# S4D convolution and gMLP mixer on one core: the cosine products of every generation unit on GpSimd, the last chunk's spectra in one part, a new instruction order

## The chip, the cores and the metric

The kernel runs on one core of a Trainium2 chip, in one launch. The metric is the device time of one execution in microseconds; runs are compared by their medians. PE is TensorE (PEld its weight loads), DVE is VectorE, ACT is ScalarE, POOL is GpSimd, SP is SyncE, which issues most of the DMAs.

## What is computed

Two residual blocks on one sequence of L = 2048 positions and D = 512 channels. The first is a diagonal state-space layer: each channel has a convolution kernel K made of 128 damped oscillations, and the layer convolves the normalized input with K by FFT. The second is a gMLP mixer with a 2048 x 2048 spatial weight.

```python
A = -exp(log_A_real) + 1j * A_imag;  C = (C_real + 1j * C_imag) * dt[:, None]
P = exp((A * dt[:, None])[:, :, None] * pos)          # 512 x 128 x 2048
K = 2 * einsum("dn,dnl->dl", C, P).real               # the generation
y = irfft(rfft(K, 4096) * rfft(u_t, 4096))[:, :L]
h = x + y + u * D_skip                                # u = layernorm(x)
z = gelu(layernorm(h) @ w_in);  z1, z2 = z[..., :896], layernorm(z[..., 896:])
out = h + (z1 * (w_sp @ z2 + b_sp)) @ w_out
```

## The kernel before

`phase_a` (lines 266 to 672) does the state-space layer up to the inverse transform over one axis; the phases `b1` to `b3` finish it and do the mixer. The change touches `phase_a` alone.

*The generation.* K is not built by exponentials of all 512 x 128 x 2048 elements. Position l is split in a coarse and a fine part, so that exp(a l) is a product of two factors with cosines and sines, and the sum over the 128 oscillations is a matmul. Each of 32 units (`unit(su)`, line 481) makes K for 16 channels:
- TensorE computes phases for the 16 channels, `c_k` times `sw` (2 matmuls of 512 columns, into a two-bank PSUM tile `ph`); ScalarE and VectorE reduce them to one turn in `cs` (part of the buffer `wb`).
- ScalarE takes the sine of all of it into a second two-bank tile, the absolute value of `cs`, and from that two cosines of 512 columns: `ce` into a PSUM bank, and `cw`.
- GpSimd makes three width factors `m` (part of `wa`, two sets, so units `su` and `su + 2` share one) out of the small tables `mt`.
- VectorE multiplies sines and width factors into `f3` (`f_94` to `f_96`). A group of 16 small matmuls, the unit's first product, starts `kp`. VectorE multiplies `ce` with two width factors in place (`wa<-ps,wa`, 1024 columns). `cw` times the third width factor is the left operand of the unit's second product, 16 more matmuls into `kp`.
- `kp` is copied to a small buffer `ks` (six of them) and GpSimd adds the skip term.

Before, where `cw` lies and who multiplies it goes by the parity of the unit (lines 499 and 525): in even units ScalarE leaves `cw` in SBUF and GpSimd multiplies (`wb<-wb,wa`), in odd units ScalarE writes it to a PSUM bank and VectorE multiplies from there (`wb<-ps,wa`).

*The transforms.* Channels come in four chunks of eight units. `piece_a` and `piece_b` transform the normalized input of a chunk (two FFT stages); `exchange` swaps the halves of its spectrum across partitions, two DMAs of 1 MB from SP, the second behind the first. `piece_c` takes the first stage of K, unit by unit, as the left operand `ks`, and evacuates to `big`. `piece_d(c, g, lo, n)` is K's second stage (left operand `big`, right operand `a2`) for the columns `lo` to `lo + n` of the eight units' 32; VectorE multiplies the result with the input's spectrum in place (`trio<-ps,trio`, always 1024 columns). `piece_e` is the inverse stage with `c_inv`: eight matmuls, which need the products of all of `piece_d` for their columns, and then an evacuation to `big` (all Q), which is what phase `b1` reads in its first matmul, `y` at line 748. The exchange of chunk c writes where `piece_e` of chunk c - 1 reads.

Before, the last chunk was split in two halves of columns, 0 to 15 and 16 to 31: four `piece_d` and four `piece_e` each. A half's `piece_d` has 8 matmuls of 64 columns, an unsplit one 4 of 128.

*What sets the order.* All of `phase_a` is first recorded (`Plan`), each instruction or group with a place in `RANKS`. `FORMS` picks the engine where a step may run on one of two (evacuations on ScalarE or VectorE, parameter steps on VectorE or GpSimd). `BANKS` picks the PSUM bank: two two-bank tiles (`ps_98`, `ps_99`) and four single banks (`ps_100` to `ps_103`). Sorted by rank, the steps are issued in that order on each engine's queue, and semaphores follow from the data. Everything recorded carries line 250 in the profile. Three tables written out as digits thus set the order; no planner runs in the kernel.

Of the kernel before, what the change touches and what calls it, by code (L numbers as in the profile page):

```python
# [12 lines left out]
AF = mybir.ActivationFunctionType  # L13
# [3 lines left out]
P = 128  # L17
# [8 lines left out]
KS_BUFS = 6  # L26
SLOT = 4096
WIDE = 2
EVERY = 2
SUC = 8  # L30
MAGIC = 12582912.0
TWO_PI = 2.0 * math.pi
# [34 lines left out]
BANKS = (
    "345242325433352143423545214452504241024301533511252002324002530153541153500454513444540422555312244155253325542112321132"
    "550042511524200223104222114331134452011043535413345514544522240544511323002434005541124251143001452201245002523545235425"
    "43212345422135332045255112430043341135311342200545113524004441124223250353252444523"  # L70
)


# [192 lines left out]
def phase_a(ctx, gen, tc, ins, cst, ident, c_mean, c_inv, Q, wp, scr):  # L266
# [214 lines left out]
    def unit(su):  # L481
# [27 lines left out]
        sn = ph[:, 1, :]  # L509
# [742 lines left out]
```

## Time and profile before

| | |
|---|---|
| median of 3 runs | 846.28 us (845.6 to 850.01) |
| the profiled execution | 844.69 us, its span 842.9 us |
| busy in the span | PE 794.1, PEld 685.6, DVE 654.2, ACT 469.1, POOL 278.5 us |
| `phase_a` ends | the first `y` matmul starts at 297.40 us |
| granted TensorE clock | full speed over nearly all of the span |

A row of a timeline has start, length, engine, line, operation, output<-input and how many instructions it merges. TensorE records two matmuls for each fp32 matmul of the program (eight `piece_e` matmuls are 16 records) and one for each phase matmul. A row that merges many instructions in close sequence is read by its length over their count. A row of the groups has busy time, mean of one in ns, and behind the second bar the idle time of the engine ahead of them with what ended it. The chain that ended last is followed back from the last instruction to whatever released each step.

### The profile page before, as it was taken

How to read it: one execution, taken by the hardware profiler on the slowest of the kernel's cores; microseconds unless marked ns; L12 is line 12 of the kernel's file. 1: busy time of each engine (PE TensorE's matmuls, PEld its weight loads, DVE VectorE, ACT ScalarE, POOL GpSimd, SP SyncE). 2: the span in 40 equal slices, each digit the busy share in tenths (PEclk: the TensorE clock that was granted, in tenths of full speed). 3: DMA queues.
4: the chain of work that ended last, by engine and by line, in shares of the span. 5: the costliest groups of instructions: out<-in, count | busy, mean ns of one | idle time of the engine just before them, and what ended most of it. 6: DMA issues, size and time to landing. Idle time of an engine off the chain costs nothing.

```text
span 842.9 us, 17463 instructions
## 1 busy us (share of the span) xinstructions
PE 794.1 (94%) x6813; PEld 685.6 (81%) x6813; DVE 654.2 (78%) x1260; ACT 469.1 (56%) x783; POOL 278.5 (33%) x332
## 2 busy tenths in 40 slices
PE   1388999999998999999999999999999999999998
PEld 0287889899997998888899988888887888888886
DVE  7999998999999488851367679988955985787633
ACT  5998999999897233543223345456534533454111
POOL 5778777787755000000042100324221002222200
PEclk9999999999999999999999999999999999999999
DMA  9231432302218676364175044899889558799832
GB/s 352 76 113 32 111 91 61 86 25 62 52 38 269 233 251 163 99 172 154 51 150 126 1 126 132 187 228 213 201 206 210 171 149 189 156 236 216 204 110 77
DMA packets 63875, 121.81 MB, mean 145 GB/s; under 512 B 6737, under 2 KB 21201, under 8 KB 61489
## 3 DMA queue, kind: packets, MB, share of 16 engines
q1 hardware_dynamic: 52160, 99.33, 38.9%
q0 software_dynamic: 11632, 21.37, 15.6%
q8 instruction: 53, 0.87, 0.4%
q14 instruction: 30, 0.24, 0.1%
HBM read 92.89 MB, written 19.40 MB: 133 GB/s over the span
## 4 chain that ended last, share of the span: by engine, by line
PE 67%; DVE 14%; DMA 7%; issue 6%; ACT 5%; POOL 1%; SPq 1%; DVEq 0%; ACTq 0%; POOLq 0%
PE ps L250 20%; PE m L1140 18%; PE pz L835 9%; PE pz L935 9%; DMA raws<-in_w_sp_dram 6%; PE po L1063 5%; DVE trio L250 4%; PE y L748 3%; PE pl L1063 2%; ACT wb L250 2%; DVE wts L676 1%; ACT big L250 1%; ACT ps L250 1%; DVE wb L250 1%; DVE f L250 1%
## 5 line engine op out<-in xcount | busy, mean ns | idle before, releaser
L1140 PE MATMUL m<-wts,zc_wa 128*128 128x512 f32 x700 | 218.0, 391 | 1.0 <-DVE c L1155 1.0
L1140 PEld LDWEIGHTS m<-wts,zc_wa 128*128 128x128 f32 x700 | 131.4, 188 | 29.8 <-DVE c L1155 1.5
L1140 PE MATMUL m<-wts,zc_wb 128*128 128x512 f32 x350 | 136.7, 391 | 0.0
L1011 POOL DMA_DIRECT2D raws<-in_w_sp_dram x64 | 58.1, 1009 | 209.2 <-DMA raws<-in_w_sp_dram 208.0
L250 POOL TENSOR_TENSOR wa<-mt 128x512 f32<-128x512 f32 x96 | 107.3, 1131 | 35.2 <-PE ps L250 15.6
L675 ACT CAST wts<-raws 128x512 fp32r<-128x512 f32 x112 | 68.8, 619 | 52.3 <-DMA raws<-in_w_sp_dram 31.7
L676 DVE TENSOR_TENSOR wts<-raws,wts 128x512 fp32r<-128x512 f32 x112 | 77.0, 690 | 19.6 <-ACT wts L675 19.5
L935 PE MATMUL pz<-w,ht 128*128 128x448 f32 x384 | 77.4, 363 | 0.0
L1140 PEld LDWEIGHTS m<-wts,zc_wb 128*128 128x128 f32 x350 | 65.7, 188 | 14.0
L935 PEld LDWEIGHTS pz<-w,ht 128*128 128x128 f32 x384 | 72.0, 188 | 5.3
L835 PE MATMUL pz<-ht,w1h 128*128 128x512 f32 x224 | 71.3, 395 | 0.0
L250 ACT ACTIVATE ps<-wb 128x512 f32<-128x512 f32 (+1 forms) x80 | 65.3, 825 | 3.4 <-DVE trio L250 1.3
L941 POOL TENSOR_SCALAR sm<-sm 128x1 f32<-128x1 f32 x16 | 5.5, 342 | 186.3 <-DVE sm L940 186.3
L250 PE MATMUL ps<-big,a 128*128 128x128 f32 (+1 forms) x512 | 62.4, 278 | 0.9 <-DVE trio L250 0.8
L675 ACT CAST zc_wa<-raws 128x384 fp32r<-128x384 f32 (+1 forms) x70 | 37.0, 533 | 46.8 <-DVE raws L1045 34.1
L1063 PE MATMUL po<-w,gz 128*128 128x512 f32 x252 | 62.6, 396 | 0.0
L250 PEld LDWEIGHTS ps<-big,a 128*128 128x128 f32 x512 | 59.3, 192 | 3.5 <-DVE trio L250 1.1
L250 PE MATMUL ps<-c_inv,trio 128*128 128x128 f32 x512 | 60.6, 277 | 1.3 <-DVE trio L250 1.3
L250 PEld LDWEIGHTS ps<-c_inv,trio 128*128 128x128 f32 x512 | 58.8, 192 | 3.2 <-DVE trio L250 1.9
L1063 PEld LDWEIGHTS po<-w,gz 128*128 128x128 f32 x252 | 47.3, 188 | 11.5 <-DVE zo L1103 0.4
L835 PEld LDWEIGHTS pz<-ht,w1h 128*128 128x128 f32 x224 | 42.1, 188 | 9.2
L1045 DVE TENSOR_TENSOR raws<-z 128x384 f32<-128x384 f32 (+1 forms) x80 | 46.1, 584 | 0.3
(162 smaller groups left out, 1533.0 us busy)
## 6 DMA issues: line engine op xcount, KB each, us to landing
raws<-in_w_sp_dram SPq DMA_DIRECT2D x112, 256.0 KB, 4.0
raws<-in_w_sp_dram POOLq DMA_DIRECT2D x80, 256.0 KB, 5.8
trio<-trio SPq DMA_DIRECT2D x8, 1024.0 KB, 6.9
g<-in_c_g_dram SPq DMA_DIRECT2D x8, 1024.0 KB, 6.7
scr_z<-zo SPq DMA_DIRECT2D x28, 256.0 KB, 2.3
big<-in_u_a_dram SPq DMA_DIRECT2D x8, 512.0 KB, 7.6
xq<-in_u_b_dram SPq DMA_DIRECT2D x4, 1024.0 KB, 6.7
scr_h<-xq SPq DMA_DIRECT2D x16, 256.0 KB, 4.9
```

What stands on the lines that cost most here:

```text
L250: r = getattr(getattr(self.nc, e), method)(*map(self.real, args), **{k: self.real(x) for k, x in kw.items()})
L675: nc.scalar.copy(hi, src)
L676: nc.vector.tensor_sub(lo, src, hi.bitcast(F32))
L748: nc.tensor.matmul(ys[n, g][:, i, :], gt[:, i, r, :], qv[:, r, l0 + i], start=(r == 0), stop=(r == 1))
L835: nc.tensor.matmul(pt, w[:, q, f], ht[n][k][:, q], start=(q == 0 and i == 0), stop=(q == 3 and i == 2))
L935: nc.tensor.matmul(pt[:, :FQ], a[:, q], w2[:, b, q, f], start=(q == 0 and i == 0), stop=(q == 3 and i == 2))
L941: nc.gpsimd.tensor_scalar_add(sm[:, 14:15], sm[:, 13:14], 1e-5)
L1011: nc.gpsimd.dma_start(r, ws[1], accum_op=ALU.add)
L1045: nc.vector.tensor_tensor(zs[:, :w], x, y, op=op)
L1063: nc.tensor.matmul(pt, gz[fb][x][:, P * a:P * a + P], wo[:, y, fb, w], start=(first and fb == fbs[0] and i == 0), stop=(last and fb == fbs ...
L1140: nc.tensor.matmul(pt, x[:, f], y, start=(k == 0 and i == 0), stop=(k == KT - 1 and i == 2))
```

## The change

Three things. In every unit `cw` stays in SBUF and GpSimd multiplies it; the PSUM bank of the odd units and their VectorE product are gone, and with them the constant `EVERY` and a branch that was never taken. The last chunk's `piece_d` and `piece_e` are recorded in one part like the other chunks': eight `piece_d` of 4 matmuls with 128 columns in place of eight with 8 of 64. And the three tables are new throughout. Line numbers fall by one where the constant is gone: recorded steps carry line 249.

```diff
-EVERY = 2
...
 RANKS = (
-    "05000608010709040B0F0A0R0M0V0I0f0Z0j03020C0E0G0H0J0K0L0O0Q0S0U0X0Y0a0N0b0d0m0g0l0o0r0u0z10121316181A1D1Y1O1a1d1h1t221w25"
...
+    "0600040901050F080B0A0b0Q0l0I0M070g0W03020C0E0G0H0J0K0L0N0O0R0V0Y0Z0c0U0d0e0n0i0m0q0t0w0z0+1112131416181J1T1w231+2628292D"
...
         nc.scalar.activation(cs, cs, AF.Abs)
-        if WIDE == 3:
-            co = nc.bank([P, 2, W], 3)
-            nc.scalar.activation(co, cs, AF.Sin, bias=half_pi, scale=-TWO_PI)
-            cw, ce = co[:, 0, :], co[:, 1:2, :]
-        else:
-            ce, cw = nc.bank([P, 1, W], 0), nc.bank([P, W], 0) if su % EVERY == 1 % EVERY else cs[:, 0, :]
-            nc.scalar.activation(ce, cs[:, 1:2, :], AF.Sin, bias=half_pi, scale=-TWO_PI)
-            nc.scalar.activation(cw, cs[:, 0, :], AF.Sin, bias=half_pi, scale=-TWO_PI)
+        ce, cw = nc.bank([P, 1, W], 0), cs[:, 0, :]
+        nc.scalar.activation(ce, cs[:, 1:2, :], AF.Sin, bias=half_pi, scale=-TWO_PI)
+        nc.scalar.activation(cw, cs[:, 0, :], AF.Sin, bias=half_pi, scale=-TWO_PI)
...
         nc.vector.tensor_mul(m[:, 0:2, :], ce.to_broadcast([P, 2, W]), m[:, 0:2, :])
-        if su % EVERY == 1 % EVERY:
-            nc.vector.tensor_mul(cs[:, 0, :], cw, m[:, 2, :])
-        else:
-            nc.gpsimd.tensor_tensor(cw, cw, m[:, 2, :], op=ALU.mult)
+        nc.gpsimd.tensor_tensor(cw, cw, m[:, 2, :], op=ALU.mult)
         with nc.group():
-            product(cs[:, 0, :], m[:, 0:2, :], 1)
+            product(cw, m[:, 0:2, :], 1)
...
-        split = [(0, 32)] if c + 1 < NCH else [(0, 16), (16, 16)]
-        for lo, m in split:
-            for g in range(NK1 // (1 << (P // m).bit_length() - 1)):
-                piece_d(c, g, lo, m)
-            for s in range(lo // 4, (lo + m) // 4):
-                piece_e(c, s)
+        for g in range(8):
+            piece_d(c, g, 0, 32)
+        for s in range(8):
+            piece_e(c, s)
```

In counts, by engine and within `phase_a`: TensorE has 2128 matmuls where it had 2160. VectorE has 454 instructions where it had 465: sixteen products fewer, four parameter steps and four `ks` copies fewer, 13 more evacuations of 512 columns. ScalarE takes as many evacuations fewer and four `ks` copies more, and loads its function table 19 times where it was 18. GpSimd has sixteen products and four parameter steps more. Everything behind `phase_a` is the same instructions in the same order.

The order at three places. First VectorE at the last two units, before. `f_94` and `f_95` are units 30 and 31; `wb<-wb,ps` reduces a unit's phases, `wa<-ps,wa` is its last multiplication, `trio<-ps,trio` a product of the last chunk's `piece_d`:

```order
L250 SCALAR_TENSOR_TENSOR wb<-wb,ps_99 128x1024
L250 TENSOR_TENSOR f_94<-ps_98,wa 128x512
L250 SCALAR_TENSOR_TENSOR f_94<-wa,ps_98 128x512
L250 COPY big<-ps_102 128x128x4
L250 TENSOR_TENSOR f_94<-ps_98,wa 128x512
L250 TENSOR_TENSOR f_95<-ps_99,wa 128x512 x2
L250 TENSOR_TENSOR wa<-ps_102,wa 128x1024
L250 TENSOR_TENSOR trio<-ps_100,trio 128x2x16x32
L250 TENSOR_TENSOR wb<-ps_102,wa 128x512
L250 SCALAR_TENSOR_TENSOR f_95<-wa,ps_99 128x512
L250 TENSOR_TENSOR wa<-ps_100,wa 128x1024
L250 TENSOR_TENSOR trio<-ps_98,trio 128x2x16x32
```

The same place now:

```order
L249 SCALAR_TENSOR_TENSOR wb<-wb,ps_99 128x1024
L249 TENSOR_TENSOR wa<-ps_102,wa 128x1024
L249 COPY big<-ps_98 128x128x4
L249 TENSOR_TENSOR f_95<-ps_99,wa 128x512
L249 SCALAR_TENSOR_TENSOR f_95<-wa,ps_99 128x512
L249 TENSOR_TENSOR f_95<-ps_99,wa 128x512
L249 TENSOR_TENSOR wa<-ps_102,wa 128x1024
L249 COPY big<-ps_101 128x128x4
L249 COPY big<-ps_102 128x128x4
L249 TENSOR_TENSOR trio<-ps_101,trio 128x64x16
L249 TENSOR_TENSOR trio<-ps_100,trio 128x64x16
```

The `wb<-ps` product of unit 31 and the `piece_d` product ahead of its last multiplication are gone; all eight `piece_d` products follow behind it, and two evacuations stand between.

Second, TensorE from the last two units to the inverse transforms of the last chunk, before (`f` and `wa,wb` are a unit's first and second product, `wb,ks` is `piece_c`, `big,a` is `piece_d`, `c_inv,trio` is `piece_e`):

```order
L250 MATMUL ps_102<-wb,ks_85 64x128 x8
L250 MATMUL ps_101<-big,a_78 128x4x16 x8
L250 MATMUL ps_100<-big,a_78 128x4x16 x8
L250 MATMUL ps_103<-big,a_78 128x4x16 x8
L250 MATMUL ps_98<-big,a_78 128x4x16 x8
L250 MATMUL ps_102<-f_94 32x64 x16
L250 MATMUL ps_102<-wa,wb 32x64 x16
L250 MATMUL ps_100<-f_95 32x64 x16
L250 MATMUL ps_100<-wa,wb 32x64 x16
L250 MATMUL ps_102<-wb,ks_80 64x128 x8
L250 MATMUL ps_100<-wb,ks_81 64x128 x8
L250 MATMUL ps_101<-c_inv,trio 128x128 x8
```

And now:

```order
L249 MATMUL ps_103<-wa,wb 32x64 x16
L249 MATMUL ps_98<-wb,ks_84 64x128 x8
L249 MATMUL ps_100<-f_95 32x64 x16
L249 MATMUL ps_100<-wa,wb 32x64 x16
L249 MATMUL ps_103<-wb,ks_80 64x128 x8
L249 MATMUL ps_102<-wb,ks_81 64x128 x8
L249 MATMUL ps_101<-big,a_78 128x4x32 x4
L249 MATMUL ps_100<-big,a_78 128x4x32 x4
L249 MATMUL ps_103<-big,a_78 128x4x32 x4
L249 MATMUL ps_102<-big,a_78 128x4x32 x4
```

Four of the eight `piece_d` stood ahead of the last two units' products; now all eight stand behind the last `piece_c`, and behind them the eight `piece_e`.

Third, TensorE at the last inverse transforms of chunk 2, which the last chunk's exchange waits for, before:

```order
L250 MATMUL ps_98<-c_k,sw_91 128x512 x2
L250 MATMUL ps_100<-c_inv,trio 128x128 x8
L250 MATMUL ps_103<-f_96 32x64 x16
L250 MATMUL ps_103<-wa,wb 32x64 x16
L250 MATMUL ps_102<-wb,ks_81 64x128 x8
```

And now:

```order
L249 MATMUL ps_100<-f_94 32x64 x16
L249 MATMUL ps_100<-wa,wb 32x64 x16
L249 MATMUL ps_98<-c_k,sw_91 128x512 x2
L249 MATMUL ps_101<-c_inv,trio 128x128 x8
L249 MATMUL ps_102<-wb,ks_82 64x128 x8
```

Before, the last inverse transform of chunk 2 stood ahead of the products of unit 26 (`f_96`); now it stands behind those of unit 27 (`f_94`), with four units still to come in place of six.

More of the change, by code (lines that the diff above doesn't have):

```diff
@@ new lines @@
+    "2E2H2K0y2J0-1K2N2P2b2X2e2V2j2u2z2p1Y1k1o2h2l2-0T0D0P0X0a0S0h0o0k0f331V371C10151W3c3N0s1O1c1r5X0j1p1l0p1j1n1q1g1D1B1U1P1m"
+    "1X1b1A0x1H0u1I1h1i0r0v1Z1G1F1a171E1Q1R1u1y222527212A2F2L2O2Q2S2U2W2Y2a2c2d2g2i3I2s3L3Y2m3K3W3M3G2w2+382v423F3Q3l2n4N3V3r"
+    "3q4P312r35323R3Z3A3D3T3y3p3O461v1f3B1-1S363E191e3C1x2t241s1z393H1N1d341M1L2q2x302M2G2o2R2I2y2k3J3P3g3k3m3X3s3t3x3z3-4043"
+    "4547494B4D4E4H4G4R4I4T544S4x4h4W4f4M4j4u4m514s4U4V5P4k4o4K4Q5H4r4e4+4X574p4L4c4J4O594Y5a5Z5T6E692C2f2Z3S3e3+414Z4d4g4i4l"
@@ new lines @@
+    "4n4t4w5A5C5I5L5U5i5n5l5s5u6P6T4A655O5R6a6l746-777A6t6r6w6+5F5M5d6I797G3b3v4C444F4b6d8u8+909194989A9L9O9d9V9f9o9kAfAhAjAv"
+    "AyB1BIAQB59GA5BOBxChCTCOCDC5CbC4CUCMC2CfCWCKCGC8CB9n9i9rAoEBEGBGEIEO555W585J4a4v5N5c5E5K4q4-52564z536U6c727C7n7s6G6N6368"
+    "6x767q7-7D7J848h3U3d3i505D5S5Y3f2T205G5B5Q5m5b5g5r608X8i8r3a3h3o5j5q5+5x3j1t2B625y5w6M6J5-6Q6V6k8E8N3n3u4y646B6S6L5o5v6C"
+    "6A6F6O6o6X6R6s707L979M3w61666i6v7873676Y6f717B6q7K7H7E7P7T7e9N9S7Q486K8m8w9T6D6W6g6n7F7W7Y6p756y6z7N7R7y7d7g818Q8a8d8o7I"
@@ new lines @@
+    "7O7V7b7h7x7v7M7Z7U7o7l7r88827z8B8G8k8x9C7f7k7u838H8L8q7t868A898C8K8-8R8z95999I9U9a7w878F8P8Z8g8l8S8M8I8c8Y8j8p8v8t92969B"
+    "9E9J7+7m8b939pA15z6b5h5p5V5f5t6H5e5k6Z6h6j6u6e6m7i7p7S7a8O8V8T8f7c7j7X808J8U858D9m9s9+A79qA2A6AA9g9vACAHA9AD9t9yAbAkAUAc"
+    "ALAnAwBNB2BFBTBcBhBsBMBkBpCZ9Z9e9lA4ABAGAK9c9Q9DAVARATAiAaAPAmArAxDBDKAFAJAMASAWAeAZ9Y9K9uAlAXAgBBAqAdBEBLBPCxD1ApAuA-B4"
+    "B6BSBCAYAsAzB7B9BDBaBUBJBdBiBrCnD4AtA+B3BVBXBjBgBABZBRBYBeBbCCBnC0CFCNCeE3ECDG9xB0BfB+EMB8BKBQBlBqCPBwBWBmBtB-BvBzC-CdCH"
@@ new lines @@
+    "D3D8DCDPDeBHCICRCcCjCvCsC9CQCXCmC+CuD5DACwDHDQDTDaDkCtCzD2D9DJDXDOCoDED6DYDNDFDjDdDbDlDsE5E8EHD7DDDSDZDgDqDmD0DVDMDrDoDi"
+    "DzDtDxE0E4E7EJESDICgDhEAETEk8W8n8e8s9F8y9H9z9P9R9W9X9b9j9hA3AEA89wA09-AIAOANBuCJBoC7CSCYCVCkCLCyC1CAByC3C6CEEcEjEVEbEYEd"
+    "EiEpEuEzEoEvEfEnElEtFlFtFdFrF3FDFSFbGTGbFKFYG1GNGHGPGcH9DfDyE2E9EDENEKERDpD-EZEQELEwEUEmEyF9FUGpGwDwE1E6ErExF7F1EXEFEaF8"
+    "F2F6FEFBF5FJFLFcGuGzEEEhFIFOFVFmFaEqF0FAFTFXFQFyFuFfF+G2G9GCGUFCFGFNFRFeFqFoFFFPFMFgFhFkFwFzFvG8GDGRGxH3FHEeFWFjGaGyFZFi"
@@ new lines @@
+    "FnFxG0G6GBFpG4GAG5GEGIGgGWGLGjGmGtHFHLFsG3G7GFGJGYGQF-GGGSGKGMGkH5GsGXH8HWHbHhHpGOGVGfGoH4HBHGH1GnGvH7H2G+HMHHHPHVHcHjHn"
+    "HvGlG-HAHIHNHYHSGdHEHKHOHRHTHdHgHeHmHoHrHtHzGrGhH6I7IDIMCiCrCqCaCpClDLDUDRDWD+DcDnDuDvEPEgEWE+F4EsE-HJHaGZGiIRIcH0HDGeGq"
+    "IOIUHQHXHwI3I0I5IFIQILISIIINIBIHI4IAI8IEIGIJIvJ2JuKCJ6JTJYJiJfJoIkJ7IYIgJNJxK2KfHZHfHkHqIKIWIPHUHsHlI2H-HyIfIbIVIiImIxKH"
+    "KNHCHiHuH+I6I9IdI1ICHxIjIXInJ0ItIhJ3J9JCKVKgITIZIeIlIpI+IuIaIsIzIqIyJ4JHJDJ1JLJOJRK0K7IrIwI-J5JBJGJQIoJ8JEJAJIJMJmJUJbJp"
@@ L70 @@
[L70 removed]
+    "345452345244335544523535253025554240055110423005311052211552013400044010433330224523313242203203321123325421144400252114"
+    "340055200435115230025311352524324022325345045255203254433350043210523113220045411434005231033511242203423245225454431323"
+    "5253334323511554004401154400223104201155200455114243534225443422535"
 )
```

34 lines of the change are left out of this document (6 added, 28 removed).

## The prediction

> **What bounds the kernel now.** I read the stretches of the execution first, then the chain that ended last, then TensorE's and VectorE's timelines around the end of the generation, and at last the grouped instructions up to 300 us. The table by stretch: its columns are the window, its length, and the busy time of PE, PEld, DVE, ACT and POOL.
>
> ```profile
> 56.00:121.50 65.50, 60.62 (x1113) 53.06 (x1105) 64.14 (x95) 61.20 (x88) 49.53 (x54) 1.00 0.40 105
> 121.50:250.00 128.50, 127.86 (x2221) 117.36 (x2223) 120.98 (x159) 119.58 (x148) 91.87 (x98) 1.00 0.23 52
> 250.00:275.00 25.00, 22.41 (x517) 19.40 (x511) 24.52 (x30) 19.90 (x29) 14.54 (x18) 1.00 0.85 260
> 275.00:297.40 22.40, 21.67 (x192) 21.48 (x192) 9.30 (x9) 6.28 (x11) 0.00 (x0) 1.00 0.53 206
> 297.40:842.90 545.50, 540.54 (x2565) 457.14 (x2565) 385.99 (x792) 217.92 (x421) 83.47 (x112) 1.00 0.64 161
> ```
>
> The change touches only what lies ahead of 297.4 us. There, three engines are nearly full at once. TensorE is busy for 127.86 of 128.5 us up to 250 us and VectorE for 24.52 of the 25 us behind that; ScalarE follows closely. GpSimd has the room: 91.87 of 128.5 us, 71%. Past 297.4 us TensorE is busy for 540.54 of 545.5 us, with an unchanged program, so I let that part move as a block. The chain that ended last (start, length, what):
>
> ```profile
> 169.00 80.70 PE ps L250 x1351
> ...
> 270.29 1.23 DVE wa L250
> 271.52 3.40 DVE trio L250 x3
> 274.97 21.72 PE ps L250 x192
> ```
>
> So the path runs through TensorE until 249.7 us, through VectorE for the last units of the generation, and through TensorE for the inverse transforms of the last chunk. The `wa` row at 270.29 us is the last multiplication of unit 31, the last unit; it ends at 271.52 us. From there to the end of the 192 matmul records, at 274.97 + 21.72 = 296.69 us, it takes 25.2 us. TensorE's timeline around this:
>
> ```profile
> 240.86 0.72 PE L250 MATMUL ps<-c_k,sw 96*128 96x512 f32 x2
> 241.42 1.95 PE L250 MATMUL ps<-c_inv,trio 128*128 128x128 f32 x16
> 243.30 0.65 PE L250 MATMUL ps<-f 128*32 128x64 f32 x32
> 243.77 0.63 PE L250 MATMUL ps<-wa,wb 128*32 128x64 f32 x32
> 244.33 2.05 PE L250 MATMUL ps<-c_inv,trio 128*128 128x128 f32 x16
> ...
> 246.67 1.95 PE L250 MATMUL ps<-c_inv,trio 128*128 128x128 f32 x16
> ...
> 263.03 7.36 PE L250 MATMUL ps<-big,a 128*128 128x64 f32 x64
> ...
> 274.97 3.84 PE L250 MATMUL ps<-c_inv,trio 128*128 128x128 f32 x32 [0.40 <-DVE trio L250]
> ...
> 287.52 9.15 PE L250 MATMUL ps<-c_inv,trio 128*128 128x128 f32 x80
> ```
>
> The row at 263.03 us is the first half of the last chunk's `piece_d`; it runs while unit 31 is still being made. The 0.40 us wait at 274.97 us is all that TensorE pays between the units and the inverse transforms.
>
> **The change, part by part.** The groups of the first 300 us (instructions, then busy us and mean ns of one, then the idle time ahead of them):
>
> ```profile
> L250 POOL TENSOR_TENSOR wa<-mt 128x512 f32<-128x512 f32 x96 | 107.3, 1131 | 35.2 <-PE ps L250 15.6 <-DVE wb L250 13.9 <-DVE trio L250 1.6
> L250 POOL TENSOR_TENSOR wb<-wb,wa 128x512 f32<-128x512 f32 x16 | 20.5, 1280 | 13.6 <-ACT wb L250 13.3 <-DVE big L250 0.2
> L250 POOL TENSOR_TENSOR ks<-ks,wb 128x4 f32<-128x4 f32 x32 | 6.6, 210 | 13.0 <-ACT ks L250 10.2 <-DVE ks L250 2.6
> L250 DVE TENSOR_TENSOR wb<-ps,wa 128x512 f32<-128x512 f32 x16 | 10.9, 684 | 0.6 <-ACT ps L250 0.5
> L250 DVE COPY ks<-ps 128x256 f32<-128x256 f32 x16 | 6.7, 418 | 0.6 <-PE ps L250 0.6
> L250 DVE TENSOR_TENSOR trio<-trio 128x128 f32<-128x128 f32 x5 | 1.5, 301 | 0.0
> L250 ACT ACTIVATE ps<-wb 128x512 f32<-128x512 f32 x48 | 32.5, 689 | 1.6 <-DVE trio L250 0.6 <-DVE wa L250 0.4
> L250 ACT ACTIVATE wb<-wb 128x512 f32<-128x512 f32 x16 | 11.5, 718 | 0.2
> L250 ACT COPY big<-ps 128x512 f32<-128x512 f32 x55 | 31.7, 580 | 18.4 <-PE ps L250 17.8
> ```
>
> And VectorE's timeline, where instructions that follow each other closely overlap by 0.08 us: the two `f` products start 0.60 us apart though each takes 0.68.
>
> ```profile
> 226.00 5.74 DVE L250 TENSOR_TENSOR trio<-ps,trio 128x1024 f32<-128x1024 f32 x5
> ...
> 239.56 1.28 DVE L250 TENSOR_TENSOR f<-ps,wa 128x512 f32<-128x512 f32 x2
> 240.76 0.68 DVE L250 TENSOR_TENSOR wb<-ps,wa 128x512 f32<-128x512 f32 x1
> ```
>
> *VectorE ahead of the last unit's multiplication.* Counted in the two orders, the sixteen `wb<-ps` products go (16 x 0.60 = 9.6 us). One `piece_d` product moves behind that point (5.74 / 5 = 1.15), four `ks` copies go to ScalarE (4 x 0.34 = 1.4) and four parameter steps to GpSimd (4 x 0.22 = 0.9). In return VectorE takes eight more evacuations of 512 columns from ScalarE (8 x 0.60 = 4.8). Sum: -13.0 + 4.8 = -8.2 us, in the stage where VectorE ends last.
>
> *ScalarE.* Sixteen sines go to SBUF for 718 ns instead of PSUM for 689 (+0.5 us), ten evacuations leave (-10 x 0.50), four `ks` copies come, and one more load of its function table: about -2 us. It was not last and stays so; I add nothing.
>
> *GpSimd.* Sixteen more products at 1280 ns are +20.5 us, the parameter steps about +1.8. Its queue idles 35.2 + 13.6 + 13.0 = 61.8 us ahead of these three groups alone, so the work fits. What is queued behind a product that waits for its sine are the width factors of later units and the `ks` additions, and VectorE and TensorE wait for those. The cost lies between 0 and the lateness worked out under the rivals; I take 0, by the 61.8 us.
>
> *The last chunk in one part.* Sixty-four records of 64 columns took 7.36 us, 115 ns each; eighty of 128 columns took 9.15 us, 114 ns each. Half the columns cost the same, so merging two halves takes away 64 records, 7.4 us of TensorE, ahead of 275 us. The price is at the end. All eight `piece_d` now stand behind the last unit, VectorE must multiply all eight before the first inverse transform, and no inverse transform of a first half is there to fill. ScalarE's copy of the last `piece_c`:
>
> ```profile
> 274.62 0.58 ACT L250 COPY big<-ps 128x512 f32<-128x512 f32 x1 [0.29 <-PE ps L250]
> ```
>
> From 271.52 to the end of this copy are 3.7 us, which stay. Then come one `piece_d` on TensorE (8 records, 0.9, and about 0.2 until VectorE starts), eight products of 1.15 (9.2) and 128 records of inverse transforms (14.6): 28.6 us where it was 25.2, so +3.4 us.
>
> *Sum*: -8.2 + 3.4 = -4.8 us, if TensorE lets VectorE run ahead. The check from TensorE's side: in the new order its last inverse transform of chunk 2 (before: ended at 246.67 + 1.95 = 248.6 us) has two more units' products and two more phase matmul pairs ahead of it: 2 x (0.47 + 0.56) + 2 x 0.56 = 3.2 us, giving 251.8. VectorE then still has twelve short and five long instructions up to unit 31's multiplication, 12 x 0.60 + 5 x 1.15 = 13.0, of which about 0.9 lie ahead: 251.8 + 12.1 + 28.6 = 292.5 against 296.7, -4.2 us. The two agree; I take -4.8. The profiled execution took 844.69 us with a span of 842.9, 1.6 us (0.2%) below the median of 846.28. Against its own time the sum gives 839.9, against the median 841.5, which is my forecast.
>
> [...]
>
> **The rivals.**
> *GpSimd holds the units up (slower).* In the odd units the second product of a unit now waits for GpSimd, 1.28 us in place of 0.68, and for what stands in its queue, one width factor of 1.13: 1.7 us late, 16 times, 27.7 us. Where half of that surfaces the kernel ends at 841.5 + 13.8 = 855.3. It is slower by over 0.5% from (4.8 + 4.2) / 27.7 = 33% on. For it: 15.6 us of GpSimd's waits already end on TensorE, because only two sets of width factors exist, and a late product delays the next set. Against it: its 61.8 idle us, and that a unit's two products stand units apart in the order. [...]
>
> *The last exchange comes late.* The two half swaps that the last `piece_d` need cannot start before chunk 2's last inverse transform:
>
> ```profile
> 248.69 7.98 SPq L250 DMA_DIRECT2D trio<-trio  x2
> ```
> ```profile
> trio<-trio SPq DMA_DIRECT2D x8, 1024.0 KB, 6.9
> ```
>
> The second is issued about 7.5 us behind the first and lands 6.9 later: 14.4 us. In the new order only units 28 to 31 stand between, 12.1 + 3.7 + 1.1 = 16.9 us. With 2.5 us of room, a TensorE that is 5 us late there costs 2.5 us: 844.0, within 0.5%.
>
> *The new order brings waits of its own.* Units 1 to 7 now follow each other with nearly equal work on all four engines; a few us of waits there, or a slower start, give 844 to 848, within 0.5%.
>
> *The start is shorter too.* Summed over the two orders with the same durations, VectorE has 1.6 us less to do ahead of the first `piece_a`, and TensorE gets chunk 1's `piece_a` earlier. If TensorE keeps 2 to 4 us of that to the end: 837.5 to 839.5.
>
> [...]
>
> **How the numbers follow.** No change here means within 0.5%, 4.2 us, about what a measurement of this kernel can tell: 842.0 to 850.5. Forecast 0.50, of it 0.40 under 842.0; shorter start 0.15; late exchange 0.10; new waits 0.13; merge without gain 0.02; GpSimd 0.10. Faster 0.40 + 0.15 = 0.55, same 0.10 + 0.10 + 0.13 + 0.02 = 0.35, slower 0.10. The range leaves out GpSimd's case and the ends of the others: 836.5 to 847.0. The forecast's own range is 839.0 to 843.5.
>
> **What would show it.** Right: unit 31's multiplication ends near 263 us, the last inverse transform near 292, VectorE's eight `trio` products stand in a row ahead of it with TensorE waiting about 3 us, and the first `y` matmul starts about 5 us earlier than at 297.4. Wrong: TensorE waiting on POOL `wb` in the units (first rival), on a DMA of `trio` ahead of the last products (second), a `piece_d` record of 128 columns at over 200 ns, or a changed length behind the first `y` matmul.

## The result, and the profile after

| | before | after |
|---|---|---|
| median | 847.29 us (845.26 to 850.01, 6 runs) | 856.37 us (853.33 to 858.88, 6 runs) |
| ratio to before, 95% interval | | 1.0105 [1.0076, 1.0134] |
| profiled execution, its span | 844.69, 842.9 us | 857.19, 855.4 us |
| first `y` matmul | 297.40 us | 309.74 us |

The change costs 1.05%, 9 us, where the forecast was a gain of 4.8. Nearly all of it lies ahead of the first `y` matmul: 12.3 of the 12.5 us between the two profiled spans. In what follows two executions of one kernel (867 and 2032 us, without the last exchange) fell in a slow state and are left out of its ratio. The stretches of the execution after, with the prediction's windows (window, length, busy time of PE, PEld, DVE, ACT and POOL, granted clock, DMA share, GB/s):

```profile
56.00:121.50 65.50, 62.47 (x1154) 56.32 (x1153) 63.64 (x90) 63.19 (x90) 52.36 (x55) 1.00 0.35 89
121.50:250.00 128.50, 120.04 (x2136) 107.41 (x2128) 117.44 (x154) 112.97 (x140) 102.46 (x106) 0.97 0.24 54
250.00:275.00 25.00, 21.91 (x454) 18.93 (x442) 22.07 (x28) 21.23 (x31) 19.73 (x22) 0.93 0.50 118
275.00:297.40 22.40, 16.10 (x177) 15.53 (x178) 9.94 (x10) 2.61 (x5) 0.21 (x1) 0.85 0.94 376
309.74:855.40 545.66, 540.28 (x2565) 456.85 (x2565) 384.99 (x790) 217.81 (x420) 83.82 (x112) 1.00 0.63 161
```

Up to 121.5 us TensorE has done 1.85 us more work than before (62.47 against 60.62 us). From there to 275 us TensorE and VectorE are both less busy than before (120.04 against 127.86 and 117.44 against 120.98 us in the second row): they wait. And the granted clock, 1.00 before, falls to 0.97, 0.93 and 0.85. TensorE's timeline, the rows with the long waits (the bracket is the idle time ahead and what ended it; "issue" means that nothing which the profile shows was waited for):

```profile
158.96 1.97 PE L249 MATMUL ps<-wb,wa 128*64 128x128 f32 x16 [5.89 <-DMA wa<-scr_xhat]
...
268.52 0.31 PE L249 MATMUL ps<-wa,wb 128*32 128x64 f32 x6 [2.84 <-issue]
...
277.43 0.87 PE L249 MATMUL ps<-f 128*32 128x64 f32 x24 [2.58 <-issue]
282.52 7.38 PE L249 MATMUL ps<-big,a 128*128 128x128 f32 x64 [0.89 <-DVE big L249]
292.88 16.19 PE L249 MATMUL ps<-c_inv,trio 128*128 128x128 f32 x128 [2.98 <-DVE trio L249]
```

The last wait, 2.98 us for VectorE's products, was forecast. The other three were not: 11.3 us. The first is for an input load of `piece_a`. The second and third stand inside a unit's product, between its 26th and 27th and its 8th and 9th record, where no semaphore stands. In or behind each of the four the clock halves, as windows laid over these places show:

```profile
157.43:164.26 6.83, 5.30 (x50) 5.30 (x52) 1.82 (x2) 3.28 (x5) 0.91 (x1) 0.50 0.28 83
...
270.07:273.48 3.41, 3.41 (x76) 2.76 (x64) 3.31 (x5) 3.26 (x5) 2.25 (x4) 0.50 0.97 221
276.90:280.31 3.41, 2.88 (x68) 2.71 (x70) 0.00 (x0) 0.37 (x1) 0.21 (x1) 0.50 1.00 418
...
293.97:297.38 3.41, 3.41 (x18) 3.41 (x17) 0.09 (x1) 1.42 (x2) 0.00 (x0) 0.50 0.74 312
```

That is 17.06 us at half speed, in which TensorE was busy for 15.0; at full speed that work would take about 7.5 us less (an estimate from these rows). The three unforeseen waits and the clock make about 18.8 us on TensorE, more than the 12.3 that surfaced.

Two theories for the waits. *SP:* SyncE's queue, before and after, around 110 to 165 us:

```profile
115.34 6.30 SPq L250 DMA_DIRECT2D scr_stk<-big  x13
121.75 0.38 SPq L250 DMA_DIRECT2D wa<-scr_xhat  x1
122.17 1.38 SPq L250 DMA_DIRECT2D scr_stk<-big  x3
...
141.06 7.29 SPq L250 DMA_DIRECT2D trio<-trio  x2
149.17 0.31 SPq L250 DMA_DIRECT2D sw<-scr_stk  x1
157.75 6.10 SPq L250 DMA_DIRECT2D wa<-scr_xhat  x4
```
```profile
136.25 0.47 SPq L249 DMA_DIRECT2D trio<-trio  x1
138.24 11.11 SPq L249 DMA_DIRECT2D scr_stk<-big  x13
149.39 0.47 SPq L249 DMA_DIRECT2D trio<-trio  x1
149.90 5.18 SPq L249 DMA_DIRECT2D scr_stk<-big  x3
155.19 0.86 SPq L249 DMA_DIRECT2D wa<-scr_xhat  x2
158.58 0.80 SPq L249 DMA_DIRECT2D sw<-scr_stk  x2
```

The sixteen writes of parameters (`scr_stk<-big`, chunks 2 and 3) were issued from 115 us on; in the new order the parameter steps that they wait for end 23 us later, and the writes hold SyncE's queue from 138 to 155 us, between the two swaps of chunk 1's exchange and ahead of the input loads `wa<-scr_xhat`, for which TensorE waits.

*FETCH:* TensorE's own instructions arrive by DMA, and it runs out of them. The trace has an `instruction` queue (q8) with one 16 KB packet at a time, 53 packets beside the 13498 matmuls and weight loads of the whole execution, one for 255; that they are TensorE's is inferred from this count. That they share DMA engines with the swaps is the theory's assumption: the trace shows their order in time. In the changed kernel none came between 254.13 and 266.23 us, though TensorE ran 547 (274 + 273) in that time:

```profile
254.13:266.23 12.10, 11.46 (x274) 9.93 (x273) 12.04 (x17) 11.93 (x16) 11.31 (x12) 1.00 0.43 89
```

The DMA queues from 257 to 266.2 us, where the first swap of the last exchange runs, then in the 0.8 us behind it, and at last from 273.2 to 275.05 us, ahead of the next block:

```profile
DMA packets 76, 1.05 MB, mean 114 GB/s; under 512 B 12, under 2 KB 12, under 8 KB 12
q1 hardware_dynamic: 76, 1.05, 55.0%
...
trio<-trio SPq DMA_DIRECT2D x1, 1024.0 KB, 6.7
...
q8 instruction: 1, 0.02, 7.5%
...
q1 hardware_dynamic: 86, 0.70, 97.2%
```

No instruction block comes in beside the swap's 64 packets of 16 KB; one comes as soon as they are done. The next block, which ends the second of these waits, starts at 275.07 us, 2 us behind the end of the second swap; in between the engines are 97% busy with 86 packets of loads, and what held this block up so long, the swap or the loads behind it, stays open. In the new order this exchange starts at 259.89 us in place of 248.69, and falls on the products of the last units, 64 records and loads in 0.47 us each. *The rival* is GpSimd, the prediction's own slower case.

### The profile page after: what moved, and what is told of

Its sections match the earlier page's. It is cut to its first block, busy times and chain, and to the rows that moved or that the text cites. A ratio compares the mean times of both kernels' runs of the same rounds, so it can differ in the third digit from the quotient of the medians.

```text
span 855.4 us, 17329 instructions
## 1 busy us (share of the span) xinstructions
PE 794.5 (93%) x6749; PEld 684.6 (80%) x6749; DVE 653.3 (76%) x1249; ACT 464.2 (54%) x775; POOL 300.8 (35%) x352
## 4 chain that ended last, share of the span: by engine, by line
PE 49%; DMA 7%; issue 4%; DVE 4%; POOL 1%; SPq 1%; ACT 1%; ACTq 0%; POOLq 0%; DVEq 0%
PE m L1129 19%; PE pz L824 9%; PE pz L924 9%; DMA raws<-in_w_sp_dram 6%; PE po L1052 4%; PE y L737 3%; PE pl L1052 2%; PE ps L249 2%; DVE wts L665 1%; DVE zc_wb L665 1%; DMA zo<-scr_h 1%; DVE c L1144 0%; DVE raws L1034 0%; DMA z1b<-scr_z 0%; POOL raws L1009 0%
## 5 line engine op out<-in xcount | busy, mean ns | idle before, releaser
L249 PE MATMUL ps<-c_inv,trio 128*128 128x128 f32 x512 | 62.8, 282 | 3.5 <-DVE trio L249 3.4
L249 PEld LDWEIGHTS ps<-c_inv,trio 128*128 128x128 f32 x512 | 60.7, 196 | 6.0 <-DVE trio L249 4.3
L249 ACT ACTIVATE wb<-wb 128x1024 f32<-128x1024 f32 (+1 forms) x64 | 56.9, 890 | 0.9
L249 ACT ACTIVATE ps<-wb 128x1024 f32<-128x1024 f32 (+1 forms) x64 | 54.5, 858 | 3.5 <-DVE wb L249 1.4
L249 PE MATMUL ps<-big,a 128*128 128x128 f32 x448 | 54.5, 278 | 1.2 <-DVE big L249 0.9
L249 PEld LDWEIGHTS ps<-big,a 128*128 128x128 f32 x448 | 51.5, 192 | 3.7 <-issue 2.6
```

Source lines behind the costliest of these rows:

```text
L249: r = getattr(getattr(self.nc, e), method)(*map(self.real, args), **{k: self.real(x) for k, x in kw.items()})
```

## The experiments

Each kernel ran beside executions of the kernel before of its own (medians 846.6 to 847.0 us), so its ratio is not its median over 847.29. An expectation that speaks of the first, second or fourth experiment means the writes later in the changed kernel, the last chunk in one part, and the writes late in the kernel before.

| kernel | median us | ratio to before, 95% interval |
|---|---|---|
| after | 856.37 | 1.0105 [1.0076, 1.0134] |
| after, writes later | 851.11 | 1.0060 [1.0036, 1.0084] |
| after, no last exchange | 849.54 | 1.0034 [1.0016, 1.0052] |
| after, last exchange in quarters | 849.79 | 1.0038 [1.0017, 1.0059] |
| after, odd units back on VectorE | 860.31 | 1.0175 [1.0150, 1.0200] |
| after, writes and quarters | 845.27 | 0.9992 [0.9973, 1.0011] |
| after, writes, quarters, kept busy | 844.82 | 0.9982 [0.9956, 1.0008] |
| before, all cosine products on GpSimd | 847.19 | 1.0008 [0.9987, 1.0030] |
| before, last chunk in one part | 852.09 | 1.0059 [1.0039, 1.0078] |
| the same, kept busy | 850.86 | 1.0041 [1.0020, 1.0063] |
| before, writes late | 844.92 | 0.9977 [0.9960, 0.9994] |
| before, last exchange in quarters | 846.20 | 1.0000 [0.9984, 1.0016] |
| before, writes late and quarters | 845.96 | 0.9988 [0.9970, 1.0006] |

**GpSimd alone, in the order before, and undone in the order after.**

```diff
-        if su % EVERY == 1 % EVERY:
-            nc.vector.tensor_mul(cs[:, 0, :], cw, m[:, 2, :])
-        else:
-            nc.gpsimd.tensor_tensor(cw, cw, m[:, 2, :], op=ALU.mult)
+        nc.gpsimd.tensor_tensor(cw, cw, m[:, 2, :], op=ALU.mult)
```


> The kernel before, in its own order, with the sixteen odd units' last product (cosine times width factor) on GpSimd out of SBUF instead of on VectorE out of PSUM; nothing else moves. Theory of the prediction (GpSimd has room): between -2 and +2 us, VectorE's busy time 10 us lower, and no wait of TensorE on POOL above 2 us in sum. Rival GpSimd: each odd unit's second product comes up to 1.7 us late, and 8 us or more of sixteen such surface as waits of TensorE on POOL wb, so +5 to +14 us, which would by itself be the changed kernel's loss of 9 us.


```diff
-        nc.gpsimd.tensor_tensor(cw, cw, m[:, 2, :], op=ALU.mult)
+        if su % 2:
+            nc.vector.tensor_mul(cw, cw, m[:, 2, :])
+        else:
+            nc.gpsimd.tensor_tensor(cw, cw, m[:, 2, :], op=ALU.mult)
```


> The changed kernel, its order and tables as they are, with the sixteen odd units' last product taken back from GpSimd to VectorE, out of SBUF. Rival GpSimd (its sixteen products of 1.28 us hold up the units in this order, if not in the order before): the time falls by 4 us or more, to 846 to 852. Theory (GpSimd is not among the causes; VectorE gets 16 x 0.6 = 9.6 us of work back, of which some surfaces near the end of the generation, where it ends last): 855 to 862.

The first came out at +0.08%, with zero inside the interval, and in its profile TensorE waits for GpSimd's product 0.5 us in all. So in the order before GpSimd's sixteen products cost nothing that these runs can tell. The second is 0.7% slower than the changed kernel, not faster: it adds VectorE's work as it takes GpSimd's away, so it does not price GpSimd alone, but taking the products back wins nothing. Its waits for the input load (5.17 us) and inside products (1.85 and 3.79 us) are there as in the changed kernel.

**The parameter writes.** In the changed kernel the eight writes of chunk 3 go behind the second swap and the input loads; in the kernel before they go behind the second swap too, but ahead of the input loads.

```diff
+MOVES = {378: 889.1, 383: 889.2, 384: 889.3, 382: 889.4, 381: 889.5, 377: 889.6, 380: 889.7, 379: 889.8}
...
+        for i, r in MOVES.items():
+            self.ops[i]["rank"] = r
```


> The changed kernel; only the eight writes of chunk 3's parameters to DRAM stand elsewhere in SyncE's queue: behind the exchange's second swap and the two input loads instead of between the two swaps. Theory SP (the new order pushed these writes in front of the input load's successor, the second swap and the next spectra, and TensorE waited 5.9 us for them at 153 us, then ran at half clock for 6.83 us): the wait falls below 1.5 us, the clock row of 0.5 at 157 us goes, and the time falls by 5.9 + 3.4 less what was hidden, to 847 to 851 from 856.4; the losses behind 250 us stay. Rival GpSimd (its sixteen more products hold the units up, and SyncE's queue had room): the wait at 153 us turns into one on POOL or ACT, and the time stays within 854 to 858. If it falls to 847 to 851, these writes alone are more than half of the change's loss.


```diff
+MOVES = {379: 866.1, 381: 866.2, 383: 866.3, 380: 866.4, 377: 866.5, 378: 866.6, 382: 866.7, 384: 866.8}
```


> The kernel before; only the eight writes of chunk 3's parameters stand later in SyncE's queue, just ahead of the tenth input load and so between the two swaps of chunk 1's exchange and the spectra that unit 16's products need, as in the changed kernel. Theory SP: TensorE waits 2 to 6 us for a DMA at about 160 us, the granted clock drops to 0.5 behind it for 3 to 7 us, and the time grows by 3 to 9 us, with the first y matmul as much later. Rival (SyncE's queue has room, the changed kernel lost its time to GpSimd or to the new order itself): within 1 us of before, clock at 1.0.

The first came out just above its expectation (851.11 against 847 to 851), with 0.45% of the 1.05% gained, less than half. SyncE's queue and TensorE of this kernel:

```profile
146.05 0.47 SPq L253 DMA_DIRECT2D trio<-trio  x1
146.56 2.78 SPq L253 DMA_DIRECT2D scr_stk<-big  x2
149.44 2.86 SPq L253 DMA_DIRECT2D wa<-scr_xhat  x2
```
```profile
151.44 0.64 PE L253 MATMUL ps<-f 128*32 128x64 f32 x28
154.87 0.31 PE L253 MATMUL ps<-f 128*32 128x64 f32 x4 [2.79 <-issue]
```

The input load starts 5.8 us earlier (149.44 in place of 155.19) and the wait for it is gone. Less than that is won, because a wait of the other kind, inside a product, came in its place: TensorE now runs its products while the swap of 146.05 us is under way.

The second missed: TensorE does not wait for the input load, the clock stays at 1.00 there, and the kernel is 0.23% faster than before, for a reason that no run shows. Its queue shows why there is no wait:

```profile
141.43 7.20 SPq L254 DMA_DIRECT2D trio<-trio  x2
149.54 0.31 SPq L254 DMA_DIRECT2D sw<-scr_stk  x1
149.91 7.17 SPq L254 DMA_DIRECT2D scr_stk<-big  x8
158.12 6.17 SPq L254 DMA_DIRECT2D wa<-scr_xhat  x4
```

In the order before, the queue has nothing to do from 150 to 158 us, and eight writes take 7.17. So theory SP holds in a narrower form: here eight writes were harmless because they fit in what the queue has free. In the changed kernel sixteen of them, 16.3 us, meet the exchange and the loads, thirteen of them between its two swaps; no run has put sixteen there in the order before.

**The last exchange.** Left out of the changed kernel, then cut in four DMAs of 512 KB, in the changed kernel and in the one before. In short:

```diff
-        return sorted(self.ops, key=lambda o: o["rank"])
+        return sorted((o for i, o in enumerate(self.ops) if i not in (1178, 1179)), key=lambda o: o["rank"])
```


> The changed kernel without the last chunk's exchange: the two swaps of 1 MB are left out, so the last chunk's spectra are multiplied unswapped. Theory FETCH (the 16 KB blocks of TensorE's instructions come through the same 16 DMA engines, a block that falls due during a swap starts only at the swap's end, and TensorE, which takes 64 instructions in 0.47 us in the units' products, runs dry): the waits of 2.84 us at 265 us and 2.58 us at 275 us inside a unit's product, both without a releaser, are gone or below 0.6 us, no half-clock rows behind them, and the time falls by 5 to 9 us, to 847 to 851 from 856.4. Rival (the waits are of the order itself, or of the engines): they stay, and the time stays within 854 to 858.


```diff
+        for i in (1178, 1179):
...
+            for k in range(2):
+                call = (e, m, (out[32 * k:32 * k + 32], src[32 * k:32 * k + 32]), kw)
...
+                if last:
+                    p["after"] = last
```


> The changed kernel; each of the last exchange's two swaps of 1 MB is issued as two DMAs of 512 KB, each behind the one before it. Nothing is left out. Theory FETCH: a block of instructions that falls due is held up by half a swap, 2.6 us, in place of 5.2 us; the two waits of 2.84 and 2.58 us inside the products shrink below 1 us, the half-clock rows behind them go, and the time falls by 4 to 8 us, to 848 to 852; the exchange lands about 4 us later, which may show as a wait of VectorE for a DMA of trio of 0 to 4 us. Rival (a block waits for the exchange as a whole, or the waits are not of the swaps): the two waits stay, and the time is 856 or above.

> The kernel before with the last exchange's two swaps each in two DMAs of 512 KB. Theory FETCH holds for the kernel before as well: some of its executions have the wait of 2.2 us inside a product at 254 us and a granted clock under 0.999, and these are its slow ones; in quarters none has it, so the median falls by 0.5 to 2.5 us and the spread from 843 to 851 narrows to 842 to 847. Rival (its spread has another source): no change, or slower by up to 4 us where the exchange, which lands later, is waited for.

Both edits of the changed kernel give nearly the same, 0.7%. Without the exchange, which the result needs, no wait of this kind is left on TensorE from 245 us on. In quarters, with nothing left out, TensorE's row that split after its 26th record in the changed kernel splits at the same record:

```profile
263.51 0.61 PE L262 MATMUL ps<-wa,wb 128*32 128x64 f32 x26
264.42 0.31 PE L262 MATMUL ps<-wa,wb 128*32 128x64 f32 x6 [0.30 <-issue]
```

The wait there is 0.30 us in place of 2.84; the second, of 2.58 us, is gone, and so are the half-clock windows behind both. In the 5 us from 258 us on, over the first of the four DMAs, a block now comes through:

```profile
q1 hardware_dynamic: 48, 0.52, 50.2%
q8 instruction: 1, 0.02, 1.2%
```

The price is a later exchange. VectorE's first product of the last chunk waits for it:

```profile
275.57 9.14 DVE L262 TENSOR_TENSOR trio<-ps,trio 128x1024 f32<-128x1024 f32 x8 [1.97 <-DMA trio<-trio]
```

So the last exchange in whole swaps is shown to cause both waits; that the first one's block comes only when the swap is done is shown by the queues, for the second it is argued. In the kernel before, quarters do not move the median. Its spread was 843.7 to 847.5 us, that of the kernel before beside it 843.3 to 851.8; twelve executions against 29 do not settle whether its longer ones have these waits.

**The last chunk in one part, alone**, in the kernel before; then with matmuls that nobody reads in TensorE's two waits.

```diff
-        split = [(0, 32)] if c + 1 < NCH else [(0, 16), (16, 16)]
+        split = [(0, 32)]
...
+        for i, r in MOVES.items():
+            self.ops[i]["rank"] = r
```


> The kernel before, with the last chunk's spectra in one part alone: the eight piece_d and eight piece_e stand at the end in the changed kernel's order, all else as before. Theory of the prediction: VectorE's end grows by 3.4 us, and it gains the two products that stood ahead of the last unit's multiplication (2 x 1.15): +1 to +3.4 us. Theory CLOCK: TensorE's wait of about 3 us ahead of the first inverse transform lowers the granted clock to 0.5 for one window of 3.4 us as it did in the changed kernel, and the product groups that now follow each other without the slow first half bring a wait of 2 to 3 us with nothing to wait for, with another such window: +5 to +9 us. Faster than before by over 1 us would refute both.


```diff
+        for r, b, n in ((1330, 3, 22), (4363.5, 1, 12)):
...
+            call = ("tensor", "matmul", (t, *self.warm), dict(start=True, stop=True))
+            self.ops.append(dict(rank=r, calls=[call] * n, names=set()))
```


> The kernel before with the last chunk in one part (the second experiment), with matmuls added whose result nobody reads: 22 where TensorE waited 6.33 us for VectorE, 12 where it waited 2.98 us ahead of the first inverse transform; one takes 0.23 us. They fill 5.1 and 2.8 us of the two waits and make no wait shorter. Theory CLOCK (the wait itself is VectorE's and costs what it costs, but the granted clock falls to 0.5 behind it for 6.83 us, which takes another 3.4): the rows of 0.5 go and the time falls by 2 to 4 us against the 852.1 of that experiment. Rival (the clock costs nothing, since VectorE sets the time there): within 1 us of it, or later by as much as the added matmuls overrun.

The first lost 0.59%, about 5 us: more than the 1 to 3.4 of the prediction's step, and the size that CLOCK gave, though not by the waits that it named. TensorE at its end, then VectorE's last multiplication of unit 31:

```profile
269.68 1.08 PE L250 MATMUL ps<-f 128*32 128x64 f32 x32 [6.33 <-DVE wb L250]
...
277.13 7.41 PE L250 MATMUL ps<-big,a 128*128 128x128 f32 x64 [0.69 <-ACT big L250]
287.52 14.56 PE L250 MATMUL ps<-c_inv,trio 128*128 128x128 f32 x128 [2.98 <-DVE trio L250]
```
```profile
270.32 1.22 DVE L250 TENSOR_TENSOR wa<-ps,wa 128x1024 f32<-128x1024 f32 x1
```

Where the first half's `piece_d` had run for 7.36 us while unit 31 was made, TensorE now waits 6.33 us for VectorE, and the products behind that take 1.08 us in place of 0.65, at half clock. The 7.4 us that the merge saves were work in a place where TensorE had to wait anyway. The multiplication ends at 271.54 us as before, and the last inverse transform at 287.52 + 14.56 = 302.08: an end of 30.5 us, where the prediction's step gave 28.6. With the added matmuls the wait for VectorE ahead of the products is 1.23 us and the last one 0.30, and the stretch from 267 to 307 us runs at full clock:

```profile
267.00:307.00 40.00, 36.48 (x484) 35.02 (x484) 26.18 (x29) 14.33 (x21) 6.04 (x8) 1.00 0.63 231
```

The time differs from the unfilled one by 0.18% with intervals that overlap: what the half clock costs there stays open. The profiled execution of this kernel also has a half-clock window of 6.83 us from 258.14 us on, behind a wait of the FETCH kind, in the part whose order is that of before, under the first swap of the last exchange:

```profile
258.45 0.85 PE L255 MATMUL ps<-f 128*32 128x64 f32 x20 [1.97 <-issue]
```

So the order before is not free of them: of the five profiled executions with this order and whole swaps, three have such a wait of 1.97 to 1.99 us there (this one, all cosine products on GpSimd, the late writes); that of the kernel before has none.

**Together.** The changed kernel with the writes later, the exchange in quarters and matmuls in the last wait; the same without these matmuls; the kernel before with late writes and quarters. The edits are those above.

> The changed kernel with three mends: the writes of chunk 3's parameters behind the second swap and the input loads (as in the first experiment), the last exchange in quarters, and 12 matmuls without a reader in TensorE's wait of 2.98 us ahead of the first inverse transform. If the causes add up (5.3 us measured for the writes, 4 to 8 for the fetches, 1.7 for half a clock window of 3.41 us), it takes 842 to 846, level with the kernel before or up to 0.5% ahead of it. If the stall at 152 us or the late exchange takes it back: 848 to 851.

> The changed kernel with the writes later and the exchange in quarters, as in the one that took 844.8 us, without the 12 matmuls ahead of the first inverse transform. Theory CLOCK (TensorE sets the time there): the granted clock falls to 0.5 for a window of 3.41 us behind the wait of 3 us, the 128 records of the last inverse transform take 16.2 us in place of 14.6, and the time is 1.2 to 2.5 us above 844.8. Rival (the clock falls but VectorE's evacuations set the time): within 0.8 us.

> The kernel before with chunk 3's parameter writes later (the fourth experiment, 844.9) and the last exchange in quarters. If both add up: 842.5 to 844.5, ahead of both kernels by 0.3% or more. If the quarters bring a wait for the exchange: 845 to 848.

The second, with the two mends and nothing added, is 1.13% faster than the changed kernel; the writes alone (0.45%) and the quarters alone (0.67%) give 1.12%. Within the intervals, each about 0.2% to either side, the two causes add up and account for the loss of 1.05%. With the added matmuls it is 844.82 us, by the interval not clearly ahead of the kernel before. In the profiles the last inverse transforms show the clock, with the matmuls and without:

```profile
280.18 14.56 PE L271 MATMUL ps<-c_inv,trio 128*128 128x128 f32 x128 [0.69 <-DVE trio L271]
295.41 9.20 PE L760 MATMUL y<-big,g 128*128 128x128 f32 x80 [0.68 <-ACT big L271]
```
```profile
280.56 16.18 PE L266 MATMUL ps<-c_inv,trio 128*128 128x128 f32 x128 [3.37 <-DVE trio L266]
297.43 9.20 PE L754 MATMUL y<-big,g 128*128 128x128 f32 x80 [0.68 <-ACT big L266]
```

The half-clock window costs 1.6 us in the row; the medians differ by 0.45 us, where CLOCK gave 1.2 to 2.5, and the ratios by 0.1%, less than either interval, so its price in the whole time stays open. The third kernel, expected at 842.5 to 844.5 if both add up, took 845.96; its interval holds both the 0.9977 of the late writes alone and 1, so whether they add up in the order before can't be told. The late writes alone are the only version here whose interval lies below the kernel before, by 0.23%.

## Why the prediction was wrong

*VectorE, 8.2 us less ahead of unit 31's last multiplication.* With both mends and the filled wait this is 6.1: the multiplication ends at 265.43 us (first row below) in place of 271.52. That profile is of the shortest execution of its kernel (841.14 us, median 844.82); without the filling the multiplication ends at 265.76, in an execution of 844.92 us. In the changed kernel it ends at 273.80, 2.3 later than before.

```profile
264.21 1.22 DVE L271 TENSOR_TENSOR wa<-ps,wa 128x1024 f32<-128x1024 f32 x1
...
270.98 9.14 DVE L271 TENSOR_TENSOR trio<-ps,trio 128x1024 f32<-128x1024 f32 x8 [1.90 <-DMA trio<-trio]
```

*The end, 28.6 us in place of 25.2.* Right in size where the clock stays full: 265.43 to 280.18 + 14.56 = 294.74 is 29.3, of which 1.9 is the wait for the quartered exchange (second row above). The sum had no term for the clock: in the order before the same end takes 30.5 us, with half clock, and there the merge costs 0.59%. In the changed kernel it is 309.07 - 273.80 = 35.3, with one wait for a block of instructions and two half-clock windows in it. That a record of 128 columns takes no longer, sixty-four in 7.38 us, is right; the 7.4 us saved bring nothing in the order before.

*GpSimd at 0, the part behind the first `y` as a block.* Both held: 1.0008 [0.9987, 1.0030] in the order before, and 545.66 against 545.50 us.

*The step that failed* is the sum's condition, "if TensorE lets VectorE run ahead", and with it the rival "the new order brings waits of its own", priced at "a few us" and 844 to 848. It was checked by counting engine work, and by the one queue entry that the last `piece_d` needs. Two things that the new order moves were not priced. The sixteen parameter writes were not followed past SyncE's queue: 5.89 us of wait, 0.45% when half of them are out of the way. And the last exchange was asked only whether it lands in time (it did, as VectorE's first product shows, which waits for TensorE and no DMA), not what runs while it is under way: 2.84 + 2.58 us of waits, 0.67% when it is cut up. The first `y` comes 12.3 us later instead of 4.8 earlier.

```profile
283.68 9.14 DVE L249 TENSOR_TENSOR trio<-ps,trio 128x1024 f32<-128x1024 f32 x8 [1.31 <-PE ps L249]
```

Without the two, and with the last wait filled, the first `y` is at 295.41 us in that shortest execution, 2.0 earlier than before, of the 4.8 forecast; without the filling it is at 297.43, level with before.

*The other rivals.* GpSimd holding the units up does not show in the order before. In the changed kernel its sign is there but small: TensorE waits 1.7 us for POOL `wb`, in two places. That this rival's 855.3 us lies next to the measured 856.37 is chance. The late exchange appeared only in quarters, at about 2 us. *Merge without gain*, 0.02 among the chances, takes a record of 128 columns to cost twice one of 64, and no run shows that: sixty-four of them took 7.38 us in the changed kernel, 115 ns each, as sixty-four of 64 columns did before (7.36 us). Of the shorter start 1.85 us of work show up to 121.5 us, less than the wait of 5.89 us at 153 us.

## What to carry to other kernels

When an order is replaced, follow every queue, SyncE's too: sum its issues between the time their inputs are ready and the next issue that somebody waits for, and compare with what the queue has free there. For each large transfer ask not only when it lands but what TensorE executes meanwhile: here small matmuls under one swap of 1 MB waited 2.84 us, until a block of instructions had come, and 0.30 us with the same swap in pieces of half the size, which let a block in between. A filler that looks like wasted work (here 64 extra records) may stand where the engine waits anyway, so its removal is worth what the trace shows behind it, not its length.

## What the runs showed of the hardware

*A wait with nothing to wait for.* Both waits inside a product of the changed kernel, of 2.84 and 2.58 us, ended 1.3 to 1.4 us after a 16 KB instruction block had come: the blocks start at 266.23 and 275.07 us and take 0.96 us, and TensorE goes on at 268.52 and 277.43. The waits began 126 matmuls and as many weight loads apart, about one block of 255; in quarters TensorE's row splits behind the same 26 records, for 0.30 us. The first swap's 64 pieces of 16 KB came in four rounds of 16, from 261.0 to 266.3 us, and the block behind the last of them; in quarters a block came between two DMAs. Why the blocks came only then no run here shows.

*The clock after waits.* In the changed kernel the clock is at 0.50 in or behind four waits of TensorE: for 6.83 us with the wait of 5.89 us, for 3.41 us each with those of 2.84, 2.58 and 2.98 us. In the kernel before, from 50 us to the first `y`, no wait is longer than 1.08 us and the clock stays at 1.00. With the last chunk in one part it is at 0.50 for 6.83 us with the wait of 6.33 us, but at 1.00 from 284.1 to 302.1 us, around the wait of 2.98 us; kept busy, that kernel has it at 0.50 for 6.83 us with a wait of 1.97 us. With writes and quarters it averages 1.00 from 121.5 to 250 us over waits of 1.36 us (kept busy) and 1.64 us (not), and 0.92 from 275 to 297.4 us around the wait of 3.37 us (not kept busy). So the length of one wait does not decide it alone: 1.97 us was enough once, 2.98 us once was not. What decides it stays open.
